# Two units of the first MoE's hidden layer moved ahead of, and beside, the last attention head's product with v

## The chip, the core and the metric

The kernel runs on one core of a Trainium2 chip. The metric is the device time of one execution in microseconds (us). All times below are of this core; the profile's clock starts at the beginning of its span.

## What is computed

Sixteen heads of masked attention (queries and keys attend only within the same cluster), then two feed-forward layers on the 1536 x 512 result.

```python
def _attn_ref(q, k, v, centroids):
    ...
    mask = q_assign[:, :, :, None] == k_assign[:, :, None, :]
    scores = scale * np.matmul(q, k.transpose(0, 1, 3, 2))
    scores = np.where(mask, scores, -1000000000.0)
    ...
    return np.matmul(attn, v)

def _moe_ref(x, w_in, w_out, a, b):
    h = x @ w_in
    P = a[0] + a[1] * h + a[2] * h2 + a[3] * h3
    Q = 1.0 + np.abs(b[0]) * np.abs(h) + np.abs(b[1]) * h2
    return (P / (Q + 1e-06)) @ w_out
```

`_moe2_ref` follows (a matmul, a softmax-weighted activation, a layer norm, a matmul). q, k and v have shape (2, 8, 768, 64); the first MoE goes 512 -> 2048 -> 512, the second 512 -> 1024 -> 512. The weights come as 64-bit floats, which the kernel turns into 32-bit ones on the way.

## The kernel before

**Attention.** Each of the 16 heads has six units of 128 query rows. A unit is a pair of score products in a two-bank PSUM tile of the tag `s` (two such tiles take turns), a minimum on VectorE (DVE, L384), an exponential on ScalarE (ACT, L397); every second unit a 32x32 block transpose on DVE (L414). The product with v (L424, 96 instructions of 64x192 a head, in a four-bank PSUM tile) of one head runs on TensorE (PE) among the units of the next. The last head has no next: its product stands alone at the end of attention. ACT copies each product out (`pv_out`, L440); that copy of head 14 must be done before head 15's product may write the same banks. For the last pair of heads the reciprocals of the row sums are spread by DVE (`rw`, L454) and turned by six PE transposes (`rbp`, L457); DVE then scales the result into `XF` (L476, L490). `XF[0..2]` are three blocks of 512 tokens; block 0 belongs to the first batch element and is complete before the last head ends.

**First MoE.** Every operand of its products is a sum of two parts, `h` and `l`, so that one product is three PE instructions: (w_h, x_h), (w_h, x_l), (w_l, x_h). A block of x is split into `XH` by four ACT copies (L325) and into `XL` by four subtractions (L612, GpSimd (POOL) for block 0). Unit u of 48 is one block of 512 tokens and one strip f of 128 of the 2048 hidden columns: `ff_h` makes h with 12 PE instructions of 128x512 (L717) in one of four PSUM banks of tag `t`; `ff_g1`, `ff_g2`, `ff_g3` put the rational function on it: ACT (L730, L731), POOL (L732, L733), DVE (L734, L735), ACT ln and exp (L741, L742), DVE (L744, L745, L746), ACT and POOL for the parts `gh` and `gl` (L751, L752). ln and exp write into h's own bank, so this bank comes free after L746. `ff_y` (L769, 12 PE instructions) adds the unit to y, which lies in both `s` tiles. Unit u + 4 needs the bank of unit u.

**Weights on the way.** Strips 0 to 4 of w_in are prepared during attention, strips 5 to 11 during units 0 to 8. A half strip is called by its strip and half here (strip 5: w50 and w51): a DMA into `raww` (SyncE's (SP) queue, L116), one ACT step (L126), a pair of DVE steps (L129, L131), then the parts `w1h` (ACT, L135) and `w1l` (POOL, L136). `raww` lies in the space of the last head's p and v, so its first DMA waits for that head's product.

**Order.** The calls are written in program order, and a scheduler in the build sets the order of each engine's queue from them; within a queue instructions start in order. `behind` adds an edge that fixes the order of two instructions on one engine. A tile is tracked as a whole: who reads one bank of a two-bank tile may be made to wait for who used the other.

Of the kernel before, what the change touches and what calls it, by code (L numbers as in the profile page):

```python
# [7 lines left out]
F32 = mybir.dt.float32  # L8
F32R = mybir.dt.float32r
# [21 lines left out]
def fused_kernel(ctx: ExitStack, tc: tile.TileContext, qT, kT, v, cent, w1, w2i, w2o, gln, coef, centT, cst, out):  # L31
# [385 lines left out]
    def pv_step(n, i):  # L417
        if i == 0:
            pv[n] = psum4(f"pv{n}")
        for c in range(2):  # L420
            j = 2 * i + c
            for r in range(4):
                sl = slice(32 * r, 32 * r + 32)
                last["pv"] = nc.tensor.matmul(  # L424
                    pv[n][64 * c:64 * c + 64, r, 0:192].rearrange("p (t q) -> p t q", t=NT),
                    lhsT=vv[n][sl, j], rhs=PT[n][sl, :, 32 * j:32 * j + 32],
                    start=(i == 0), stop=(i == S // 64 - 1),
                )

    U, W = {}, {}  # L430

# [185 lines left out]
    for idx, (n, t) in enumerate(units):  # L617
        if idx == ACL:
            asg.close()
            wh["r"] = ctx.enter_context(tc.tile_pool(name="wh2", bufs=4, side="right"))  # L620
        for k in range(3, len(sets)):
            if idx == AT[k] - LD:
                load_pairs(sets[k])
        if t == 0:
            if n + 2 < B * H:
                load_head(n + 2)
            if n >= 1 and n + 1 < B * H:
                spread(prep_head(n + 1), 7, idx, idx + 6)
        if t == 2:
            load_v(n)  # L630
        sp = unit_scores(n, t)
        m = unit_max(n, t, sp)
        if t % 2 and idx > 1:
            turn_p(*divmod(idx // 2 - 1, NT // 2))
        if idx == S1A:
            set1_a()
        if idx == S1B:
            set1_b()

        if n and t >= 3:  # L640
            for i in range(4 * (t - 3), 4 * (t - 2)):
                pv_step(n - 1, i)
            if t == 5 and n % 2 == 0:
                pair_sums(n // 2 - 1)
        unit_exp(n, t, sp, m)
        if n >= 2 and t < 2:
            pv_out(n - 2, t)
            if t == 1 and n % 2:

                fin_ = pair_fin(n // 2 - 1)  # L650
                for i in (1, 5, 6, 7):
                    plan[min(96, idx + i)].append(fin_)
        run_plan(idx)
    for i in range(2):
        pv_out(B * H - 2, i)
    turn_p(B * H - 1, NT // 2 - 1)
    pair_sums(B * H // 2 - 1)
    for i in range(NS):
        pv_step(B * H - 1, i)
    for i in range(2):  # L660
        pv_out(B * H - 1, i)
    XHL = xy.tile([128, 9, 512], F32R, name="xhl", tag="x")
    XH, XL = XHL[:, 0:4], XHL[:, 4:8]
    for _ in split_x(0, nc.scalar, nc.gpsimd):
        pass
    for _ in pair_fin(B * H // 2 - 1):
        pass
    for _ in range(3):
# [37 lines left out]
    def ff_h(u):  # L706
        j, f = ff_units[u]
        xh, xl = XH, XL
        w_h, w_l = w1_t[f]
        if u and u % 8 == 0 and (f == 0 or j < 2):  # L710
            for _ in split_x(j, nc.scalar, nc.vector):
                pass
        hp = psum1(f"h{u}")
        i = 0
        for kt in range(4):
            for w, x in ((w_h, xh), (w_h, xl), (w_l, xh)):
                r = nc.tensor.matmul(hp, lhsT=w[:, kt * 128:(kt + 1) * 128], rhs=x[:, kt], start=(i == 0), stop=(i == 11))  # L717
                if u < 4 and i == 0:
                    behind(r, last["pv"])
                i += 1  # L720
        return hp
# [267 lines left out]
```

## Time and profile before

| what | us |
|---|---|
| median of 3 runs | 711.69 |
| lowest and highest run | 710.28, 712.29 |
| the profiled execution's own time | 711.83 |
| its span in the profile | 710.0 |
| PE busy in the span | 617.8 (87%) |
| DVE busy | 528.8 (74%) |
| ACT busy | 409.6 (58%) |
| POOL busy | 399.5 (56%) |

The span is what the profile shows from the first instruction to the last; 1.8 us of the profiled execution lie around it. Matmuls are pipelined, so a busy PE is not PE at its peak. The chain that ended last lies on PE for 39% of the span, on DVE for 13%, on POOL for 3%, on ACT for 2% and on DMA for 1%. The granted clock of TensorE has two levels, 2.4 GHz (1.00 in the rows) and 1.2 GHz (0.50). The stretch that the change touches goes from 257 us, where the last exponential ends, to about 300 us.

### The profile page before, as it was taken

The page shows a single profiled execution, that of the slowest core. Times are in us where ns is not written, and L with a number is a line of the kernel's source. Part 1 is how long each engine was busy: PE and PEld are TensorE (multiplying, and loading weights), DVE is VectorE, ACT ScalarE, POOL GpSimd, SP SyncE. Part 2 cuts the span into 40 slices and gives each one's busy share as a digit, 9 for nine tenths or more (in the row PEclk, how much of TensorE's full clock was granted, in tenths as well). Part 3 has the DMA queues.
Part 4 walks back from the last instruction along what each step waited for, and adds up shares of the span by engine and source line. Part 5 has one row for each costly group of instructions (what it writes and reads, how often), then busy time and mean ns, then how long its engine had stood idle before and what let it go on. Part 6 is the DMA issues. An engine that isn't in the chain of part 4 may idle for free.

```text
span 710.0 us, 13783 instructions
## 1 busy us (share of the span) xinstructions
PE 617.8 (87%) x5517; PEld 487.6 (69%) x5517; DVE 528.8 (74%) x695; ACT 409.6 (58%) x748; POOL 399.5 (56%) x363
## 2 busy tenths in 40 slices
PE   6777876687688778599999999899979999999998
PEld 3555655565466556478788878678858888888887
DVE  4779798898978854999866999987677765444450
ACT  2536554665557644887757777758556544444341
POOL 8555447383758743999856999897669500000000
PEclk9779999899789889799999999999989999999999
DMA  9964393855747304323100234230010000000001
GB/s 258 257 168 102 91 257 112 209 144 142 178 127 173 85 25 159 137 90 120 60 1 0 87 120 124 87 118 1 0 31 0 1 1 15 31 30 15 18 28 44
DMA packets 22439, 64.71 MB, mean 91 GB/s; under 512 B 4532, under 2 KB 5640, under 8 KB 22376
## 3 DMA queue, kind: packets, MB, share of 16 engines
q1 hardware_dynamic: 21944, 63.67, 32.0%
q8 instruction: 43, 0.70, 0.4%
q10 hardware_dynamic: 432, 0.17, 0.1%
q14 instruction: 20, 0.16, 0.1%
HBM read 59.16 MB, written 3.19 MB: 88 GB/s over the span
## 4 chain that ended last, share of the span: by engine, by line
PE 39%; DVE 13%; issue 4%; POOL 3%; ACT 2%; DMA 1%; SPq 0%; ACTq 0%; POOLq 0%; DVEq 0%
PE y L769 10%; PE o L896 9%; PE hh L845 9%; PE h L717 8%; DVE y L734 2%; DVE w1w L131 2%; DVE q L744 2%; DVE h L745 2%; PE lt L878 1%; DVE y L746 1%; DVE y L735 1%; DVE w1w L129 1%; DVE xhl L612 1%; POOL q L733 1%; DMA raww<-in_w 1%
## 5 line engine op out<-in xcount | busy, mean ns | idle before, releaser
L717 PE MATMUL h<-xhl,w1h 128*128 128x512 f32 x384 | 126.8, 406 | 20.5 <-DVE y L746 17.3
L397 ACT ACTIVATE p<-s,m 128x768 f32<-128x768 f32 x96 | 86.0, 898 | 83.1 <-DVE m L384 82.6
L384 DVE TENSOR_REDUCE m<-s 128x1 f32<-128x768 f32 x96 | 89.0, 942 | 30.2 <-PE s L379 29.9
L373 PE MATMUL s<-k,q 128*128 128x384 f32 x192 | 63.8, 418 | 48.1 <-ACT p L397 47.6
L717 PEld LDWEIGHTS h<-xhl,w1h 128*128 128x128 f32 x384 | 74.2, 195 | 40.9 <-DVE y L746 20.1
L424 PE MATMUL pv<-pt,v 32*64 32x192 f32 x3072 | 86.8, 363 | 3.1 <-issue 2.9
L414 DVE STREAM_TRANSPOSE pt<-p 128x1536 f32<-128x1536 f32 x48 | 84.5, 1762 | 0.0
L373 PEld LDWEIGHTS s<-k,q 128*128 128x128 f32 x192 | 33.1, 210 | 72.7 <-ACT p L397 55.2
L424 PEld LDWEIGHTS pv<-pt,v 32*64 32x64 f32 x3072 | 65.9, 148 | 20.6 <-issue 15.2
L769 PE MATMUL y<-gl,w1h 128*128 128x512 f32 x192 | 75.6, 394 | 1.5 <-POOL gl L752 1.5
L717 PE MATMUL h<-xhl,w1l 128*128 128x512 f32 x192 | 76.5, 400 | 0.0
L752 POOL TENSOR_TENSOR gl<-y,gh 128x512 fp32r<-128x512 f32 x48 | 66.9, 1393 | 14.7 <-ACT gh L751 14.6
L769 PE MATMUL y<-gh,w1l 128*128 128x512 f32 x192 | 75.1, 391 | 0.0
L769 PE MATMUL y<-gh,w1h 128*128 128x512 f32 x192 | 68.7, 392 | 0.2 <-ACT yp L785 0.2
L733 POOL TENSOR_TENSOR q<-q,t 128x512 f32<-128x512 f32 x48 | 66.7, 1389 | 2.8
L732 POOL TENSOR_SCALAR q<-t,ab 128x512 f32<-128x512 f32 x48 | 48.4, 1009 | 27.6 <-ACT t L730 18.8
L379 PE MATMUL s<-k,q 128*128 128x384 f32 x192 | 55.9, 378 | 2.3 <-DVE k L575 2.3
L741 ACT ACTIVATE h<-q,qc 128x512 f32<-128x512 f32 x48 | 33.2, 692 | 36.6 <-POOL q L733 29.0
L734 DVE TENSOR_TENSOR y<-y,h 128x512 f32<-128x512 f32 x48 | 32.7, 680 | 28.4 <-ACT y L731 28.3
L845 PE MATMUL hh<-vh,xhl 128*128 128x512 f32 x192 | 53.2, 391 | 0.0
L490 POOL TENSOR_TENSOR xf<-u,rb 128x512 f32<-128x512 f32 (+1 forms) x14 | 13.9, 1016 | 64.2 <-DMA rb<-rd 64.2
L769 PEld LDWEIGHTS y<-gl,w1h 128*128 128x128 f32 x192 | 36.1, 188 | 10.7 <-POOL gl L752 2.9
(151 smaller groups left out, 1358.4 us busy)
## 6 DMA issues: line engine op xcount, KB each, us to landing
raww<-in_w SPq DMA_DIRECT2D x32, 512.0 KB, 4.2
v<-in_v SPq DMA_DIRECT2D x64, 192.0 KB, 4.7
dup<-in_qT SPq DMA_DIRECT2D x31, 192.0 KB, 5.6
dup<-in_kT SPq DMA_DIRECT2D x31, 192.0 KB, 5.1
rawv<-in_w2i SPq DMA_DIRECT2D x8, 512.0 KB, 3.7
rawv<-in_w2o SPq DMA_DIRECT2D x8, 512.0 KB, 4.0
out<-ob SPq DMA_DIRECT2D x11, 256.0 KB, 2.0
pr<-in_qT SPq DMA_DIRECT2D x7, 384.0 KB, 6.0
```

The lines of the kernel that those rows point to most:

```text
L373: r = nc.tensor.matmul(sp[:, a, 0:384], lhsT=q1[i][:, sl], rhs=k1[i][:, a * 384:(a + 1) * 384], start=True, stop=False)
L379: last["pe"] = nc.tensor.matmul(sp[:, a, 0:384], lhsT=q2[i][:, sl], rhs=k2[i][:, a * 384:(a + 1) * 384], start=False, stop=True)
L384: last["dve"] = nc.vector.tensor_reduce(m, sp[:, :, 0:384], axis=AX.XY, op=ALU.min)
L397: last["act"] = nc.scalar.activation(out=P[n, t // 2][:, t % 2], in_=sp[:, :, 0:384], func=AF.Exp, scale=-1.0, bias=m, accum_out=rs[key][: ...
L414: r = nc.vector.transpose(PT[n][:, 2 * i:2 * i + 2].rearrange("p t k -> p (t k)"), p.rearrange("p t a k -> p (t a k)"))
L424: last["pv"] = nc.tensor.matmul(pv[n][64 * c:64 * c + 64, r, 0:192].rearrange("p (t q) -> p t q", t=NT), lhsT=vv[n][sl, j], rhs=PT[n][sl, ...
L717: r = nc.tensor.matmul(hp, lhsT=w[:, kt * 128:(kt + 1) * 128], rhs=x[:, kt], start=(i == 0), stop=(i == 11))
L733: nc.gpsimd.tensor_tensor(q, q, t, op=ALU.mult)
L752: nc.gpsimd.tensor_tensor(gl, y, gh.bitcast(F32), op=ALU.subtract)
L769: nc.tensor.matmul(o, lhsT=w[:, c], rhs=g, start=(first and i == 0), stop=(last and i == 2))
L845: last["th"] = nc.tensor.matmul(hp[:, a], lhsT=y[:, kt], rhs=w[:, 512 * a:512 * a + 512], start=(kt == 0 and e == 0), stop=(kt == 3 and e ...
L896: r = nc.tensor.matmul(op[:, 0:m], lhsT=l[:, kt], rhs=w, start=(n == 0), stop=(n == 23))
```

## The change

The h of units 0 and 1 goes into one two-bank tile of tag `s`, called `early`, instead of two `t` banks. Block 0 of x is split right after the last unit, ahead of the copies of head 14's product; half of the `XL` subtractions go from POOL to DVE. The eight products of unit 0 with `XH` are put ahead of the last head's product with v, its four products with `XL` and the 12 of unit 1 behind it. `pair_sums`, which makes `rw` and `rbp`, is written behind them. In `ff_h`, units 0 and 1 return the bank that is already filled, and the edge to the last product with v now holds for units up to 5.

```diff
     def pv_step(n, i):
...
+        before = last["pv"] if i == 0 and n == B * H - 1 else None
...
+                if before:
+                    behind(last["pv"], before)
+                    before = None
...
+    XHL = xy.tile([128, 9, 512], F32R, name="xhl", tag="x")
+    XH, XL = XHL[:, 0:4], XHL[:, 4:8]
+    early = psum2("s", "h01")
+
+    def early_h(u, i0, i1):
+        w_h, w_l = w1_t[u]
+        ps_ = [(w, XH, kt) for kt in range(4) for w in (w_h, w_l)] + [(w_h, XL, kt) for kt in range(4)]
+        for i in range(i0, i1):
+            w, x, kt = ps_[i]
+            r = nc.tensor.matmul(early[:, u], lhsT=w[:, kt * 128:(kt + 1) * 128], rhs=x[:, kt], start=(i == 0), stop=(i == 11))
+            behind(r, last["pv"])
+            last["pv"] = r
+
+    for kt in range(4):
+        rnd(nc.scalar, XH[:, kt], XF[0][:, kt])
+    early_h(0, 0, 8)
     for i in range(2):
         pv_out(B * H - 2, i)
     turn_p(B * H - 1, NT // 2 - 1)
-    pair_sums(B * H // 2 - 1)
+    for kt in range(4):
+        (nc.gpsimd, nc.vector)[kt // 2].tensor_tensor(XL[:, kt], XF[0][:, kt], XH[:, kt].bitcast(F32), op=ALU.subtract)
     for i in range(NS):
         pv_step(B * H - 1, i)
+    early_h(0, 8, 12)
+    pair_sums(B * H // 2 - 1)
     for i in range(2):
         pv_out(B * H - 1, i)
-    XHL = xy.tile([128, 9, 512], F32R, name="xhl", tag="x")
-    XH, XL = XHL[:, 0:4], XHL[:, 4:8]
-    for _ in split_x(0, nc.scalar, nc.gpsimd):
-        pass
+    early_h(1, 0, 12)
...
+        if u < 2:
+            return early[:, u]
...
-                if u < 4 and i == 0:
+                if u < 6 and i == 0:
                     behind(r, last["pv"])
```

On PE, at the end of attention, the queue before reads as follows (`pv14`, `pv15` are the products of heads 14 and 15, `h0` the h of unit 0; what a row waits for stands in brackets, by the engine or DMA semaphore):

```order
L424 MATMUL pv14_3165<-pt14_2985,v14_2960 64x192 x32
L457 MATMUL rbp_3290<-cst_70,rw_3288 128x128 [waits DVE_49,Activation_49]
L457 MATMUL rbp_3290<-cst_70,rw_3288 128x128 x5
L424 MATMUL pv15_3297<-pt15_3163,v15_3141 64x192 [waits DMAHW3_49,PE_49,Activation_49]
...
L424 MATMUL pv15_3297<-pt15_3163,v15_3141 64x192 x92
L717 MATMUL h0_3465<-xhl_3396,w1h0_2537 128x512 [waits PE_49,Activation_49]
```

and with the change (`h01` is the tile `early`):

```order
L425 MATMUL pv14_3165<-pt14_2985,v14_2960 64x192 x32
L669 MATMUL h01_3282<-xhl_3281,w1h0_2537 128x512 [waits Activation_49]
L669 MATMUL h01_3282<-xhl_3281,w1l0_2538 128x512
L461 MATMUL rbp_3409<-cst_70,rw_3407 128x128 [waits DVE_49,PE_49]
L461 MATMUL rbp_3409<-cst_70,rw_3407 128x128 x5
L669 MATMUL h01_3282<-xhl_3281,w1h0_2537 128x512 [waits Activation_49]
L669 MATMUL h01_3282<-xhl_3281,w1l0_2538 128x512
...
L425 MATMUL pv15_3304<-pt15_3163,v15_3141 64x192 [waits DMAHW3_49,PE_49,Activation_49]
...
L425 MATMUL pv15_3304<-pt15_3163,v15_3141 64x192 x92
L669 MATMUL h01_3282<-xhl_3281,w1h0_2537 128x512 [waits Pool_49] x2
```

Two of the eight early products stand ahead of the transposes `rbp`, six stand between these and head 15's product, and the rest of units 0 and 1 behind it.

On ACT, at the start of the first MoE, the queue before reads (`t0`, `y0` are the first two ACT steps of unit 0, `t1` the first of unit 1; `h0<-q0` and `h0<-h0` are ln and exp of unit 0):

```order
L126 ACTIVATE w1w51_3487<-raww151_3488 128x512 [waits DMAHW3_49]
...
L126 ACTIVATE w1w60_3528<-raww160_3529 128x512 [waits DMAHW4_49,Pool_49]
L730 ACTIVATE t0_3478<-h0_3465 128x512 [waits DMAHW1_49,DMAHW5_49,DMAHW0_49,PE_49]
L731 ACTIVATE y0_3480<-h0_3465,coef_72 128x512
...
L730 ACTIVATE t1_3513<-h1_3500 128x512 [waits PE_49,Activation_49,Pool_49]
L731 ACTIVATE y1_3515<-h1_3500,coef_72 128x512
L741 ACTIVATE h0_3465<-q0_3479,qc_3449 128x512 [waits DVE_49]
...
L742 ACTIVATE h0_3465<-h0_3465 128x512 [waits Activation_49]
```

and with the change:

```order
L126 ACTIVATE w1w51_3499<-raww151_3500 128x512 [waits DMAHW3_49]
L135 ACTIVATE w1h5_3480<-w1w50_3482 128x512 [waits DMAHW5_49,DMAHW4_49,DMAHW6_49,DMAHW1_49,DMAHW7_49,DMAHW0_49,DVE_49]
L754 ACTIVATE t0_3490<-h01_3282 128x512 [waits DMAHW0_49,DMAHW1_49,PE_49,DMAHW5_49,Activation_49,Pool_49]
...
L765 ACTIVATE h01_3282<-q0_3491,qc_3474 128x512 [waits Pool_49]
L135 ACTIVATE w1h6_3525<-w1w61_3580 128x512 [waits DVE_49]
L766 ACTIVATE h01_3282<-h01_3282 128x512 [waits Activation_49]
...
L135 ACTIVATE w1h7_3631<-w1w70_3633 128x512 [waits DVE_49]
L754 ACTIVATE t1_3512<-h01_3282 128x512 [waits DVE_49]
L755 ACTIVATE y1_3514<-h01_3282,coef_72 128x512
L775 ACTIVATE gh0_3521<-y0_3492 128x512
```

`t0` has moved ahead of w60's step; `t1` has moved from ahead of unit 0's ln to behind its exp and behind the DVE steps of w70. The DVE instruction that `t1` waits for is L770 of unit 0 (L746 in the kernel before), the last of that unit on DVE.

## Rows read from the trace of the kernel before

**Rows 1.** Busy time by stretch: us, busy us (instructions) of each engine, clock, DMA.

```profile
280.00:300.00 20.00, 11.35 (x43) 8.89 (x42) 19.67 (x27) 16.11 (x28) 18.28 (x15) 0.74 0.40 134
300.00:346.00 46.00, 43.69 (x187) 34.28 (x185) 44.15 (x60) 34.35 (x59) 43.52 (x33) 1.00 0.32 110
```

**Rows 2.** The chain that ended last, in order of time: start, us, what.

```profile
263.14 6.43 PE pv L424 x192
...
269.98 6.53 DMA raww<-in_w
...
282.17 0.68 DVE y L734
...
312.51 1.04 DVE xhl L612
...
467.48 2.73 PE h L717 x12
```

**Rows 3.** PE's timeline: start, us, instruction, count [idle before, what ended it].

```profile
255.25 1.56 PE L424 MATMUL pv<-pt,v 32*64 32x192 f32 x64
261.62 1.51 PE L457 MATMUL rbp<-cst,rw 128*128 128x128 f32 x6 [4.82 <-DVE rw L454]
...
291.20 1.22 PE L717 MATMUL h<-xhl,w1h 128*128 128x512 f32 x2 [8.65 <-DVE y L746]
...
292.65 1.05 PE L717 MATMUL h<-xhl,w1h 128*128 128x512 f32 x2
...
293.93 1.05 PE L717 MATMUL h<-xhl,w1h 128*128 128x512 f32 x2
...
301.73 0.62 PE L717 MATMUL h<-xhl,w1h 128*128 128x512 f32 x2
```

**Rows 4.** PE alone by stretch: us, busy us (instructions), granted clock, DMA.

```profile
260.00:261.00 1.00, 0.00 (x0) 0.93 0.00 0
267.00:268.00 1.00, 1.00 (x47) 0.66 0.00 0
284.00:285.00 1.00, 0.00 (x0) 0.88 0.85 303
```

**Rows 5.** ACT's timeline.

```profile
257.58 0.79 ACT L440 ACTIVATE u<-pv 64x768 f32<-64x768 f32 x1
...
259.10 2.17 ACT L325 ACTIVATE xhl<-xf 128x512 fp32r<-128x512 f32 x4
...
276.53 0.66 ACT L126 ACTIVATE w1w<-raww 128x512 f32<-128x512 f32 x1 [1.72 <-DMA raww<-in_w]
...
280.13 0.58 ACT L730 ACTIVATE t<-h 128x512 f32<-128x512 f32 x1
...
283.42 0.60 ACT L730 ACTIVATE t<-h 128x512 f32<-128x512 f32 x1 [0.50 <-POOL q L733]
```

**Rows 6.** DVE's timeline.

```profile
290.41 0.73 DVE L746 SCALAR_TENSOR_TENSOR y<-y,coef,h 128x512 f32<-128x512 f32 x1
...
295.35 0.73 DVE L746 SCALAR_TENSOR_TENSOR y<-y,coef,h 128x512 f32<-128x512 f32 x1
...
299.24 0.73 DVE L746 SCALAR_TENSOR_TENSOR y<-y,coef,h 128x512 f32<-128x512 f32 x1
...
303.77 0.67 DVE L744 SCALAR_TENSOR_TENSOR q<-q,h 128x512 f32<-128x512 f32 x1
304.37 0.73 DVE L735 SCALAR_TENSOR_TENSOR y<-y,coef,h 128x512 f32<-128x512 f32 x1
305.03 0.68 DVE L745 SCALAR_TENSOR_TENSOR h<-q,h 128x512 f32<-128x512 f32 x1
...
311.78 0.73 DVE L746 SCALAR_TENSOR_TENSOR y<-y,coef,h 128x512 f32<-128x512 f32 x1
```

**Rows 7.** POOL's timeline.

```profile
281.80 1.58 POOL L733 TENSOR_TENSOR q<-q,t 128x512 f32<-128x512 f32 x1
...
293.40 1.47 POOL L752 TENSOR_TENSOR gl<-y,gh 128x512 fp32r<-128x512 f32 x1
```

## The prediction

> **What bounds the kernel now.** First the busy time by stretch. From 280 to 300 us DVE is busy 19.67 of 20 us and PE 11.35; from 300 to 346 both are nearly full, PE 43.69 and DVE 44.15 of 46 [rows 1]. So early in the first MoE, PE has time to spare, and soon neither has. Then the chain of waits: the last head's product with v (263.14 to 269.57), the DMA of half strips of weights (the second lands at 276.51), then DVE instruction after instruction past 312.51 [rows 2]. PE's own rows show what the change aims at: a gap of 4.82 us before `rbp`, and one of 8.65 us before unit 4's h at 291.20, which waits for unit 0's L746, the last reader of its bank [rows 3].
>
> What the reader should see: the filled gaps are PE's, while the chain runs over the DMA and DVE. PE work moved into a gap is worth only what it makes DVE do earlier.
>
> **Part 1, up to the last product with v.** Before, ACT's two copies of head 14 stand ahead of the split, from 257.58; the four `XH` copies start at 259.10, one every 0.54 us (2.17 over 4) [rows 5]. With the order turned round the first `XH` is there at about 258.2 and the fourth at 259.8. Then come head 14's copies (1.52 us, from 257.58 to 259.10), done by 261.3, before anybody needs them. Two early products run at 258.3. The third stands behind `rbp`, which starts at 261.62 and ends at 263.13 as before, for DVE's `rw` is not earlier [rows 3]. So 4.8 us of gap take only 0.5 us of work; six products fall between `rbp` and head 15.
>
> Their price depends on the clock. In 260 to 261 the granted share is 0.93, so it fell to the lower level at 260.86; in 267 to 268 it is 0.66, so it rose at 267.68 [rows 4]. At the lower level the products of this shape go one in 0.43 us (three from 292.65 to 293.93 [rows 3]), so six take 2.56; at the upper one 0.23 (12 in 2.73 [rows 2]), so 1.37. I take the lower level: PE stands nearly idle in that gap still. Head 15 then starts at 265.69. Of its product 1.9 us lay after the rise before; at 24.4 ns each (64 in 1.56 [rows 3]) that is 77 of the 192. From 265.69 to 267.68 some 51 are done at the slow pace (115 in 4.54 us), and 141 at 24.4 ns take 3.44. End: 271.1 instead of 269.57, **+1.6 us**.
>
> The first weight DMA waits for that end, and so the second lands at 278.1. SP's queue has the same order as before.
>
> **Part 2, unit 0.** The remaining 16 products end at 274.8. In front of `t0` ACT has w51's first step at the landing (278.1 to 278.8) and one copy, so `t0` starts at 279.2, against 280.13 [rows 5], though all inputs are later: it passed w60's step in the queue. L758 (L734 before) starts on DVE at 280.45, against 282.17 [rows 2], 1.7 us earlier. But it passed a DVE pair too. From 282.17 to 312.51 DVE ran 41 instructions in 30.34 us: 16 at 0.60 and 11 at 0.66 (the distances of starts in [rows 6]), 16.9 us, and seven pairs in the other 13.5, so 1.93 a pair. Passing one leaves **+0.2 us**.
>
> **Part 3, the wait that comes in.** `t1` now waits for unit 0's last DVE instruction, and it stands on ACT behind unit 0's exp. Followed through the queues: on POOL w51's subtraction stands between the two steps of q; it starts behind w51's copy (281.0) and q's first step and ends at about 283.0, and at 1.4 to 1.6 us a step [rows 7] q is ready at 284.4, against 283.38. On ACT the exp stands behind w61's copy, which needs DVE until 285.8 (two pairs behind L759 at 281.8); the exp ends at 287.0, and DVE stands idle for 1.25 us. With two strip steps in between, unit 0 leaves DVE at 291.8, against 291.14 [rows 6]. `t1` starts there, against 283.42 [rows 5]. Behind it ln waits for POOL's q, which waits for `t1`; DVE idles for another 0.3, 0.45 and 0.2 us. Unit 1 leaves DVE at 300.9, unit 2 at 307.0, unit 4 at 317.0, against 296.08, 299.97 and 312.51 [rows 6]. Not all of that is loss, since DVE has done strip work meanwhile: at unit 4's end one pair more, 1.93 us, is behind it, so the lag is 2.6, and the idle time alone says **+2.2 us** on top of part 2.
>
> This term was never measured. Its lower end is 0 (`t1` delayed, but DVE always has strips to do), its upper end 4.8 (unit 1's lag in full). I take 2.2, nearest to the counted idle time.
>
> Here the Trainium skill speaks against me. Its page "PSUM — Partial Sum Buffer" (section "Specifications (TRN2)") says ScalarE and VectorE can access PSUM in parallel at full rate as long as there is no bank collision, and h of units 0 and 1 lie in two banks; by it the term would be 0 and the sum +0.2. No run here shows that; the wait stands in the order, so the rule has no hold on it.
>
> **PE's side, as a check.** Unit 6's h needs the bank of unit 2: 307.0 instead of 301.73 [rows 3], with ten more products of y done by then (2.3 us): +3.0. Units 4 and 5 did run early, up to 286.7, but `ff_y` of unit 0 waits for `gl`, 296.2 instead of 294.87 [rows 7], and its second half for the tile `early`, so for unit 1, until 300.9. The gap is moved, not closed.
>
> **Edits at no cost.** Two subtractions on DVE after `rw` lie in time that DVE spent waiting for head 15's copies; at 0.67 each, as its other steps of this shape [rows 6], they would cost 1.3 us without that cover. POOL keeps two of four, so it is done earlier. Head 15's copies and the scaling into `XF` are 1.6 us later, and nothing reads these before block 1's split at 312.51 [rows 2]. The wait of the next h for the copies is hidden behind 16 products (3.7 us). The wider edge (up to unit 5) only fixes an order that holds anyway.
>
> **Sum.** 0.2 + 2.2 = 2.4 on DVE's side, 3.0 on PE's; I take 2.6, since the chain runs on DVE first. Behind that both are as full as before, so nothing gives it back. 711.83 + 2.6 = 714.4 against the profiled execution, 714.3 against the median of the runs, which is 0.14 lower. Farther on the scheduler has also changed many places by one or two instructions; I cost that at nothing and bound it by one pair, 1.9 us, either way. About 0.3% (2.1 us) is what a measurement of this kernel tells from no change.
>
> **Rivals.**
> *The clock holds* (0.18). The two early products at 258.3 break the gap, and it may be that the clock stays up. For it: before, PE did nothing at all there. Against: it also fell at 284.76, with the share at 0.88 from 284 to 285 [rows 4], 2.2 us after products that had kept PE full. Then head 15 starts at 264.5 and ends after 4.7 us at 269.2, 1.9 us earlier than in part 1: 714.4 - 1.9 = 712.5. In the words of the Trainium skill ("TensorE: Matmul & The Clock Gate", section "Part 1: The HAM clock gate (the "warmup" mystery)") the slow state is the default and activity releases it, by which either can come; no run here shows it.
>
> *PE was the bound, and the gap does close* (0.15, the other side). From 300 to 346 PE has 2.3 us to spare [rows 1]; with the h of units 4 and 5 taken out, 5.5 us, DVE alone sets the pace. It gains the 1.7 us of an earlier L758 and its own 1.85 us of idle time: 711.83 - 3.55 = 708.3. It decides at unit 1: if that leaves DVE by 296 as before, this holds. Against it is the place of `t1` in the queue.
>
> *No change* (0.15). The delay is there, but the units after the last strip take it back, since DVE has time again there: 711.8. Against: in 300 to 346 POOL is as full as PE (43.52 us [rows 1]), and both wait for the late units.
>
> **Numbers.** Forecast 0.52, at 712.9 to 717.5. Its upper end is 711.83 + 0.2 + 4.8 and some 0.7 of the later places; the lower end of all that is no gain on DVE's side is 711.83 - 1.9, about 710. Range 710.0 to 717.5; most of the faster rival lies below it. Slower by over 2.1 us: four fifths of the forecast and a little of the clock's case, 0.46. Faster: 0.14. The rest, 0.40, within 0.3%.
>
> **What would show it.** Right: the last product with v ends near 271, the clock is at 0.50 at 262; DVE's first L758 at 280 to 281; `t1` after unit 0's L770, at 291 to 292; unit 1's L770 at 300 to 301; PE idle from 287 to 293 and again before 301. Wrong: unit 1's L770 before 297, or the product with v ending by 269.5, or DVE idle for less than 1 us from 281 to 308.

## The result and the profile after

The changed kernel takes 720.79 us (median of 4 runs, 716.05 to 721.42), the kernel before on the same chip 711.52 (4 runs, 710.28 to 712.29). The ratio is 1.0114 with a 95% interval of 1.0081 to 1.0148; by the medians it is 9.3 us more. The forecast was 2.6 us more, with a range up to 717.5.

| us | before | after |
|---|---|---|
| the profiled execution | 711.83 | 721.42 |
| its span | 710.0 | 719.6 |
| PE busy, share of the span | 617.8, 87% | 624.3, 87% |
| DVE busy | 528.8 | 532.8 |
| ACT busy | 409.6 | 408.8 |
| POOL busy | 399.5 | 393.5 |
| the row that closes the last exp starts at | 257.14 | 259.17 |
| from there to the end of the span | 452.9 | 460.4 |

The last two lines matter for every date below. Up to the last exp no instruction moved, and still it closed 2.03 us later in this profile. In the 17 profiles of this study that row starts anywhere from 254.95 to 261.18. So dates are counted from it here, and times are compared by ratios. Even so two profiles of one order differ: from that row to the end the change takes 460.4 and, run again (e1), 461.9 us, the kernel before 452.9 and, with the same order written out (e15), 451.1. A difference of under 2 us between two profiles shows nothing by itself.

First the stretches that answer to [rows 1], 2 us later as the last exp is. The columns are the window, its length, then busy time and instructions of PE, its weight loads, DVE, ACT and POOL, the granted clock, the DMA share and GB/s.

```profile
282.00:302.00 20.00, 8.86 (x28) 5.99 (x28) 18.49 (x23) 13.47 (x23) 16.14 (x13) 0.71 0.42 143
302.00:348.00 46.00, 41.74 (x169) 32.58 (x168) 43.68 (x60) 34.93 (x60) 41.75 (x33) 0.94 0.31 104
```

PE was meant to gain here. It is busy 8.86 of 20 us instead of 11.35, since its early work is done and the next waits; DVE lost 1.2 us.

PE's own rows, which answer to [rows 3] (start, length, what ran, and in brackets the idle time before it and what ended it):

```profile
260.28 0.50 PE L669 MATMUL h<-xhl,w1h 128*128 128x512 f32 x1 [1.45 <-ACT xhl L325]
...
263.38 1.51 PE L461 MATMUL rbp<-cst,rw 128*128 128x128 f32 x6 [2.36 <-DVE rw L458]
264.54 0.78 PE L669 MATMUL h<-xhl,w1h 128*128 128x512 f32 x1
...
266.93 4.27 PE L425 MATMUL pv<-pt,v 32*64 32x192 f32 x192
...
292.80 0.80 PE L793 MATMUL y<-gh,w1h 128*128 128x512 f32 x1 [6.72 <-ACT gh L775]
295.90 0.80 PE L793 MATMUL y<-gl,w1h 128*128 128x512 f32 x1 [2.31 <-POOL gl L776]
300.52 0.80 PE L793 MATMUL y<-gh,w1h 128*128 128x512 f32 x1 [2.12 <-DVE y L770]
307.64 0.73 PE L741 MATMUL h<-xhl,w1h 128*128 128x512 f32 x2 [1.16 <-DVE y L770]
```

The gap of 8.65 us before unit 4's h is gone and has come back as 6.72 + 2.31 + 2.12 us before y of units 0 and 1. From the end of the product of head 14 (its last rows start at 257.28) to 302 us PE is idle 14.95 us of 44.72, before, from 255.25 to 300, 15.27 of 44.75. The early products moved PE's idle time and did not lessen it.

ACT's and DVE's rows on the way there, which answer to [rows 5] and [rows 6]; first ACT:

```profile
279.06 0.59 ACT L754 ACTIVATE t<-h 128x512 f32<-128x512 f32 x1
...
290.96 0.60 ACT L754 ACTIVATE t<-h 128x512 f32<-128x512 f32 x1 [0.41 <-DVE y L770]
```

and DVE:

```profile
280.35 0.69 DVE L758 TENSOR_TENSOR y<-y,h 128x512 f32<-128x512 f32 x1 [0.52 <-ACT y L755]
...
287.38 0.69 DVE L768 SCALAR_TENSOR_TENSOR q<-q,h 128x512 f32<-128x512 f32 x1 [1.33 <-ACT h L766]
...
290.19 0.74 DVE L770 SCALAR_TENSOR_TENSOR y<-y,coef,h 128x512 f32<-128x512 f32 x1
```

`t1` does start 0.03 us behind unit 0's last DVE step. Unit 4's last step ends at 316.57, which is 57.40 us behind the last exp, against 55.37 before: 2.0 us later, with one pair of strip steps more done (11 L131 steps by then, before 10). At unit 7 it is 2.7 us, again with one pair more. The rest of the loss comes later, and PE's rows there show some of it:

```profile
328.27 1.22 PE L741 MATMUL h<-xhl,w1h 128*128 128x512 f32 x2 [2.67 <-DVE y L770]
...
413.21 0.72 PE L741 MATMUL h<-xhl,w1h 128*128 128x512 f32 x2 [0.75 <-DVE y L770]
417.30 0.73 PE L741 MATMUL h<-xhl,w1h 128*128 128x512 f32 x2 [0.60 <-DVE y L770]
431.14 0.73 PE L741 MATMUL h<-xhl,w1h 128*128 128x512 f32 x2 [0.34 <-DVE y L770]
436.15 0.72 PE L741 MATMUL h<-xhl,w1h 128*128 128x512 f32 x2 [1.54 <-DVE y L770]
454.24 0.74 PE L741 MATMUL h<-xhl,w1h 128*128 128x512 f32 x2 [1.41 <-DVE y L770]
470.65 0.84 PE L741 MATMUL h<-xhl,w1h 128*128 128x512 f32 x2 [2.93 <-DVE y L770]
```

The six from 413 on add up to 7.57 us; before, the six gaps from 418 to 463 us add up to 4.61:

```profile
418.55 0.74 PE L717 MATMUL h<-xhl,w1h 128*128 128x512 f32 x2 [0.69 <-DVE y L746]
422.59 0.50 PE L769 MATMUL y<-gl,w1h 128*128 128x512 f32 x1 [0.53 <-POOL gl L752]
445.63 0.73 PE L717 MATMUL h<-xhl,w1h 128*128 128x512 f32 x2 [0.59 <-DVE y L746]
455.80 0.50 PE L717 MATMUL h<-xhl,w1h 128*128 128x512 f32 x1 [0.71 <-DVE xhl L612]
460.36 0.50 PE L717 MATMUL h<-xhl,w1h 128*128 128x512 f32 x1 [0.63 <-DVE xhl L612]
462.55 1.22 PE L717 MATMUL h<-xhl,w1h 128*128 128x512 f32 x2 [1.46 <-DVE y L746]
```

Nothing that the change names stands there. But the scheduler has put the later queues in another order, and that is the suspicion that the experiments follow.

### The profile page after: what moved, and what is told of

Its sections match the earlier page's. It is cut to its first block, busy times and chain, and to the rows that moved or that the text cites. A ratio compares the mean times of both kernels' runs of the same rounds, so it can differ in the third digit from the quotient of the medians.

```text
span 719.6 us, 13781 instructions
## 1 busy us (share of the span) xinstructions
PE 624.3 (87%) x5517; PEld 490.5 (68%) x5517; DVE 532.8 (74%) x697; ACT 408.8 (57%) x748; POOL 393.5 (55%) x361
## 4 chain that ended last, share of the span: by engine, by line
PE 40%; POOL 8%; DVE 8%; ACT 3%; issue 3%; DMA 1%; SPq 0%; ACTq 0%; POOLq 0%; DVEq 0%
PE y L793 10%; PE hh L869 9%; PE o L920 9%; PE h L741 9%; POOL q L757 2%; POOL gl L776 2%; PE lt L902 1%; POOL q L756 1%; POOL w1l L136 1%; DVE w1w L131 1%; POOL vl L136 1%; DVE q L768 1%; DVE xhl L616 1%; DMA raww<-in_w 1%; DVE y L770 1%
## 5 line engine op out<-in xcount | busy, mean ns | idle before, releaser
L741 PE MATMUL h<-xhl,w1h 128*128 128x512 f32 x368 | 119.3, 401 | 12.0 <-DVE y L770 12.0
L373 PE MATMUL s<-k,q 128*128 128x384 f32 x192 | 64.5, 422 | 48.4 <-ACT p L397 47.6
L741 PEld LDWEIGHTS h<-xhl,w1h 128*128 128x128 f32 x368 | 69.9, 192 | 31.0 <-DVE y L770 15.8
L425 PE MATMUL pv<-pt,v 32*64 32x192 f32 x3072 | 84.7, 356 | 2.3 <-issue 2.1
L793 PE MATMUL y<-gl,w1h 128*128 128x512 f32 x192 | 77.8, 405 | 4.1 <-POOL gl L776 4.1
L793 PE MATMUL y<-gh,w1h 128*128 128x512 f32 x192 | 71.0, 403 | 11.8 <-ACT gh L775 9.7
L793 PE MATMUL y<-gh,w1l 128*128 128x512 f32 x192 | 76.8, 400 | 0.0
L741 PE MATMUL h<-xhl,w1l 128*128 128x512 f32 x184 | 72.9, 397 | 0.0
L757 POOL TENSOR_TENSOR q<-q,t 128x512 f32<-128x512 f32 x48 | 68.2, 1420 | 2.6
L756 POOL TENSOR_SCALAR q<-t,ab 128x512 f32<-128x512 f32 x48 | 45.4, 947 | 29.4 <-ACT t L754 22.4
L758 DVE TENSOR_TENSOR y<-y,h 128x512 f32<-128x512 f32 x48 | 32.7, 682 | 29.8 <-ACT y L755 29.7
L793 PEld LDWEIGHTS y<-gh,w1h 128*128 128x128 f32 x192 | 37.0, 193 | 21.3 <-ACT gh L775 10.5
```

Source lines behind the costliest of these rows:

```text
L373: r = nc.tensor.matmul(sp[:, a, 0:384], lhsT=q1[i][:, sl], rhs=k1[i][:, a * 384:(a + 1) * 384], start=True, stop=False)
L425: last["pv"] = nc.tensor.matmul(pv[n][64 * c:64 * c + 64, r, 0:192].rearrange("p (t q) -> p t q", t=NT), lhsT=vv[n][sl, j], rhs=PT[n][sl, ...
L757: nc.gpsimd.tensor_tensor(q, q, t, op=ALU.mult)
L793: nc.tensor.matmul(o, lhsT=w[:, c], rhs=g, start=(first and i == 0), stop=(last and i == 2))
```

## The experiments

Two theories to begin with. **A**: the early products and the wait of `t1` cost it, and later stages only pass the delay on. **B**: the early part costs what was forecast, and the rest is the new order of the units behind it. Beside them stands **C**: a part of it is chance in the attention stage. All ratios are to the kernel before, run beside.

| run | us | ratio | 95% interval |
|---|---|---|---|
| e1 the change again | 721.7 | 1.0156 | 1.0131 to 1.0180 |
| e2 no early products | 707.05 | 0.9943 | 0.9922 to 0.9963 |
| e3 unit 0 only | 715.68 | 1.0071 | 1.0049 to 1.0093 |
| e4 ln and exp to SBUF | 720.75 | 1.0135 | 1.0109 to 1.0160 |
| e5 the change, order of e2 | 709.18 | 0.9973 | 0.9950 to 0.9997 |
| e6 the change, order of before | 716.45 | 1.0055 | 1.0029 to 1.0081 |
| e7 e2, order of the change | 721.94 | 1.0154 | 1.0123 to 1.0185 |
| e8 before, order of e2 | 705.23 | 0.9904 | 0.9878 to 0.9930 |
| e9 unit 0 only, order of before | 714.74 | 1.0034 | 1.0013 to 1.0054 |
| e10 unit 0 only, order of e2 | 708.89 | 0.9951 | 0.9928 to 0.9975 |
| e11 six products behind | 717.66 | 1.0079 | 1.0051 to 1.0108 |
| e12 before, four DVE steps moved | 712.0 | 0.9998 | 0.9970 to 1.0026 |
| e13 order of before, units 8 to 15 | 718.51 | 1.0106 | 1.0072 to 1.0140 |
| e14 order of before, from 16 on | 716.63 | 1.0093 | 1.0057 to 1.0128 |
| e15 before, its order written out | 710.64 | 1.0000 | 0.9976 to 1.0023 |

**e1: the same again.** No edit.

> The changed kernel once more, nothing edited, for the spread of its time and of its stages. Theory A (the wait of t1 for unit 0 and what hangs on it set the loss) and theory B (the new order of instructions behind unit 7, which the scheduler chose, costs most of it) both expect 719 to 722 us, and the same idle times of TensorE as in the first profile: 6.7, 2.3 and 2.1 us before 302 us, and about 5 us more than before between 302 and 572. Theory C (part of the loss is chance: the attention stage took 2.0 us longer in the first profile though its order is unchanged) expects the last exp to start anywhere from 256 to 259 us and the time to move with it, with a median of 717 to 719.

721.7 us. Here the last exp closed 2.3 us earlier than in the first profile (256.89), but the rest took 461.9 us, so the time stayed. PE's gaps were 6.99, 2.19 and 2.13 us. Theory C is out as a cause of the loss.

**e2: no early products.** The other edits stay.

```diff
-    early_h(0, 0, 8)
...
-    early_h(0, 8, 12)
...
-    early_h(1, 0, 12)
...
-        if u < 2:
-            return early[:, u]
```

> The change without the early products: h of units 0 and 1 computed where they were before, in banks of their own, the other edits (block 0 of x split ahead of the copies, two subtractions on VectorE) kept. Theory A expects no loss: 711 to 713 us, t1 within 5 us of t0, unit 1's last VectorE step near 296 us. Theory B expects 715 to 718, because the scheduler orders the later units anew for this edit too, with TensorE idle 4 to 6 us more than before between 302 and 572.

Neither theory had this: 707.05, faster than before by 0.6%. Up to unit 7 it is level with the changed kernel (78.0 and 78.6 us behind the last exp), and then it wins 13.5 us. That spoke for B, with an order that can also be better than the one before. Up to unit 7 e2 is not level with the kernel before, though: that stood at 75.9 there, and at 74.3 to 75.6 in three more profiles with its early order (e8, e12, e15). The section on why the prediction failed comes back to this.

**e3: unit 0 only.**

```diff
-    early_h(1, 0, 12)
...
-        if u < 2:
+        if u < 1:
+            turn[0] += 1
             return early[:, u]
```

> The changed kernel with h of unit 0 alone in the score banks; unit 1 has a bank of its own as before, so t1 waits for nothing of unit 0. Theory A expects 712 to 715 us: t1 about 4 us behind t0, no idle VectorE from 281 to 308, unit 1's last VectorE step at 295 to 298 us. Theory B expects 716 to 720, with unit 1 as early as A says, and the loss behind 317 us.

715.68. ACT's rows: `t1` has a bank of its own and starts at 280.70, 3.5 us behind `t0`:

```profile
277.19 0.58 ACT L754 ACTIVATE t<-h 128x512 f32<-128x512 f32 x1
...
280.70 0.60 ACT L754 ACTIVATE t<-h 128x512 f32<-128x512 f32 x1 [1.17 <-POOL q L757]
```

Unit 1's last DVE step ends 33.9 us behind the last exp (before 38.9), unit 5's 54.1 (before 63.5). A part of that lead is strip work put off (8 pairs done by unit 4, before 10), and all of it is gone at unit 20 (149.8, before 145.7). The dates are as B had them; the time lies between A's range and B's.

**e4: ln and exp into SBUF**, so that nobody writes over `early`.

```diff
         q, y, r = live[u]
+        if u < 2:
+            r = T("r", u)
```

> The changed kernel with both units early, but the result of ln and exp of units 0 and 1 written to a tile in SBUF instead of over h, so that t1 waits for nothing of unit 0 and the score banks come free with unit 1's second product on VectorE. Theory A expects a gain: 708 to 713 us, VectorE's idle time of 1.3 us gone, unit 1's last VectorE step by 297 us, y of units 0 and 1 begun by 296 us. Theory B expects 715 to 719 in spite of that.

720.75, no gain: above the ranges of both theories, and against A, though not a clean test of it. The wait for unit 0's last step is gone, but the scheduler leaves `t1` on ACT behind unit 0's ln, and DVE is idle for it as before. ACT:

```profile
283.80 0.71 ACT L767 ACTIVATE r<-q,qc 128x512 f32<-128x512 f32 x1
284.41 0.57 ACT L754 ACTIVATE t<-h 128x512 f32<-128x512 f32 x1
```

and DVE:

```profile
285.69 0.69 DVE L758 TENSOR_TENSOR y<-y,h 128x512 f32<-128x512 f32 x1 [1.40 <-ACT y L755]
```

**e5 to e8: the order by itself.** Everything from unit 7's ln on is written in the same sequence in all these kernels: 1680 matmuls, 401 DVE, 380 ACT, 158 POOL instructions and 42 DMAs. Their order in the queues can therefore be taken from one kernel and given to another, by an edge between neighbours on each engine that fixes the order and waits for nothing (the tables of numbers and their unpacking are left out; `p_` is the order of an engine, `l_` its instructions as written):

```diff
+        if u == 8:
+            mark[0] = len(nc.cur_bb.bb.instructions)
...
+        for i_ in nc.cur_bb.bb.instructions[mark[0]:]:
+            mine.setdefault(str(i_.engine).split(".")[-1], []).append(i_)
+        for e_, (n_, s_) in ORDER.items():
...
+            for a_, b_ in zip(p_, p_[1:]):
+                tc.add_manual_dep(l_[b_], l_[a_].name, mybir.DependencyInfo(mybir.DependencyClass.NoSync, mybir.DependencyReason.DATA), reason="order")
```

Between the changed kernel and e2, 556 of the matmuls, 193 DVE, 211 ACT and 89 POOL instructions stand in another place, and none of the DMAs.

> The changed kernel, early products and all; only the order of what is written from unit 7's ln on is fixed, on all five engines, to the order that the scheduler gave the kernel without early products (707 us). Theory B (the later order costs it) expects 705 to 710 us: up to unit 7 the two kernels had stood level (78.6 and 78.0 us behind the last exp), and from there each stage should last as in the kernel without early products. Theory A (the early products cost it, later stages only pass the delay on) expects 717 to 722, as the changed kernel.

> The changed kernel with the order of the kernel before from unit 7's ln on. Theory B expects what step by step was forecast for the early part alone: 711 to 715 us. Theory A expects 717 to 722.

> The kernel without early products (707 us), with the changed kernel's order from unit 7's ln on. Theory B expects the loss to move over to it: 717 to 722 us. Theory A expects 705 to 710.

> The kernel before, with the order of the kernel without early products from unit 7's ln on. Theory B expects a gain without any edit of the work: 704 to 709 us, TensorE's idle time before its last VectorE result at 529 us (4.7 us) gone. Theory A expects 710 to 713.

709.18, 716.45, 721.94 and 705.23. Three of the four lie in B's range and none in A's; e6 lies between the two. The changed kernel with e2's order is no slower than before, e2 with the changed kernel's order is as slow as the change, and the kernel before with e2's order is 1% faster than itself. The kernel before with the changed kernel's order was not run.

The dates show how. Each number is the end of that unit's last DVE step behind the row that closes the last exp; the last column is the end of the span.

| | unit 4 | unit 7 | unit 15 | unit 23 | unit 31 | unit 39 | unit 47 | end |
|---|---|---|---|---|---|---|---|---|
| before | 55.4 | 75.9 | 116.6 | 166.6 | 213.7 | 258.5 | 307.5 | 452.9 |
| after | 57.4 | 78.6 | 120.2 | 171.9 | 222.2 | 263.1 | 308.1 | 460.4 |
| e6 | 57.9 | 79.3 | 120.0 | 170.1 | 217.2 | 262.0 | 311.2 | 456.7 |
| e5 | 56.6 | 78.5 | 118.6 | 165.1 | 219.3 | 257.3 | 300.3 | 448.5 |
| e2 | 57.1 | 78.0 | 116.0 | 163.0 | 217.3 | 255.2 | 298.3 | 446.3 |
| e7 | 54.6 | 79.7 | 122.5 | 174.2 | 224.5 | 266.7 | 311.7 | 462.9 |
| e8 | 53.4 | 74.9 | 115.2 | 161.6 | 215.9 | 253.9 | 296.9 | 445.0 |

e6 reads the early part apart from the later order: with the order of before it is 3.5 us behind at unit 7, 3.5 at unit 23, 3.7 at unit 47 and 3.8 at the end. Against e15, the other profile of that order, it is 5.0, 5.0, 5.3 and 5.6. So a delay from the early part passes through unchanged, neither taken back nor grown, and its size is known to some 2 us. And with one order a stage lasts the same whatever came ahead. From unit 23 to 31 and from 31 to 39, before:

```profile
423.74:470.86 47.12, 43.73 (x181) 34.21 (x180) 44.86 (x64) 35.13 (x61) 43.01 (x34) 0.96 0.38 112
470.86:515.59 44.73, 44.73 (x197) 36.57 (x196) 33.04 (x49) 28.93 (x48) 32.66 (x28) 1.00 0.08 24
```

e6, the order of before:

```profile
426.99:474.11 47.12, 43.73 (x180) 34.10 (x179) 44.89 (x64) 35.16 (x61) 43.01 (x34) 0.96 0.37 112
474.11:518.91 44.80, 44.80 (x197) 36.77 (x197) 33.22 (x49) 28.96 (x48) 32.65 (x28) 1.00 0.08 24
```

after, in its own order:

```profile
431.09:481.35 50.26, 44.33 (x184) 35.41 (x185) 49.47 (x64) 35.89 (x63) 46.55 (x37) 0.97 0.38 112
481.35:522.27 40.92, 40.92 (x181) 33.64 (x180) 31.41 (x47) 29.68 (x51) 29.38 (x26) 1.00 0.06 18
```

Between two orders the dates of units do not say where time is lost, since the work between them differs: the second of these stages is 3.8 us shorter after the change, with 181 PE instructions in it instead of 197, and at unit 47 the change is 0.6 us behind, with 727 PE instructions still to come instead of 697. PE's idle time says it. From the last exp to the end every kernel here has the same 2046 PE instructions. The sums over that stretch (its length, then busy time of each engine) are, for before, e6, after and e5:

```profile
sum 452.86, PE 423.06 PEld 344.75 DVE 315.80 ACT 268.27 POOL 242.68; mean PE 47.01 PEld 38.31 DVE 35.09 ACT 29.81 POOL 26.96
sum 456.69, PE 426.15 PEld 345.46 DVE 316.90 ACT 267.69 POOL 237.31; mean PE 47.35 PEld 38.38 DVE 35.21 ACT 29.74 POOL 26.37
sum 460.43, PE 425.95 PEld 345.88 DVE 321.86 ACT 267.61 POOL 236.74; mean PE 47.33 PEld 38.43 DVE 35.76 ACT 29.73 POOL 26.30
sum 448.47, PE 420.88 PEld 343.37 DVE 321.20 ACT 267.98 POOL 236.06; mean PE 46.76 PEld 38.15 DVE 35.69 ACT 29.78 POOL 26.23
```

From e6 to after, PE's busy time stays (426.15 and 425.95) and its idle time grows from 30.5 to 34.5 us (35.0 in e1): what the changed kernel's later order costs is 4 us of idle PE. From e6 to e5 PE has 3.0 us less idle time and 5.3 less busy time, at a granted clock of 0.97 and 0.98. From before to e6 idle time goes from 29.8 to 30.5 and busy time grows by 3.1 (against e15, by 2.5 and 3.0): a good part of what the early part costs is PE's work at the lower clock. From unit 0's last DVE step to unit 4's the granted clock is 0.91 before and 0.69 in e6 (columns as at the top):

```profile
291.14:312.51 21.37, 21.31 (x85) 17.38 (x86) 21.30 (x31) 16.96 (x29) 21.18 (x16) 0.91 0.33 113
290.37:314.85 24.48, 18.11 (x57) 13.12 (x58) 24.11 (x33) 19.23 (x33) 23.87 (x20) 0.69 0.38 126
```

In the stage from unit 23 to 31 DVE has 64 instructions in both orders, but they take 49.47 us instead of 44.86. DVE's groups in it, before and after, say which (busy time, mean ns of one, idle time):

```profile
L131 DVE SCALAR_TENSOR_TENSOR vw<-rawv,vw 128x512 uint32<-128x512 uint32 x10 | 10.1, 1013 | 0.0
```

```profile
L131 DVE SCALAR_TENSOR_TENSOR vw<-rawv,vw 128x512 uint32<-128x512 uint32 x10 | 13.4, 1341 | 0.1
```

The same ten steps take 3.3 us more. The stage is 3.1 us longer, and the six PE gaps from 413 us on add up to 3.0 us more. That the steps make the gaps is not shown: e5 has as much busy DVE time as the change (321.20 and 321.86) and is fast. Why ten equal steps differ stands in the last section.

**e9 and e10: the shared tile by itself**, e3 with the order of before and with that of e2.

> Only unit 0 early, unit 1 in a bank of its own, with the order of the kernel before from unit 7's ln on; to be set against both units early at that order (716.5 us, 3.8 us behind before in the profile). If the forecast's third part is right (t1 waits for unit 0, because the two units share one tile), that delay goes with the shared tile: 711 to 713 us, unit 4's last VectorE step 51 to 53 us behind the last exp instead of 57.9. If the delay has another cause in the early part (weight pairs passed, the clock), it stays: 715 to 718.

> Only unit 0 early, with the order of the kernel without early products from unit 7's ln on; both units early at that order took 709.2 us. If the shared tile is what costs: 704 to 707. If not: 708 to 711.

714.74 lies just under the range for another cause, 708.89 in it: both above what was expected if the tile were all of it. Unit 4 did leave DVE 50.7 us behind the last exp, about as expected, instead of e6's 57.9, but with 8 pairs of strip steps done instead of 10; at unit 7, with 14 pairs in both, 2.6 us of these 7.2 were left, and 2.8 at the end (453.9 against 456.7). By the ratios the second unit in the shared tile costs 1.5 us at the order of before (1.0055 and 1.0034) and 1.6 at e2's (0.9973 and 0.9951), both with intervals that overlap. So it is a part of the early loss at most, and not shown to be the larger one.

**e11: six products behind.**

```diff
-    early_h(0, 0, 8)
+    early_h(0, 0, 2)
...
-    early_h(0, 8, 12)
+    early_h(0, 2, 12)
```

> The changed kernel with the six early products between the transposes of rbp and the last product with v moved behind it; the later order is almost that of the changed kernel. The forecast's first part (six products at the lower clock delay the product with v by 1.6 us) expects 719 to 720 us against 720.8 to 721.7. By the first profiles, where the product with v ended no later after the last exp than before (12.1 us against 12.4), no difference: 720 to 722.

717.66. By the ratios that is 2.5 us under the change, with intervals that overlap, and 5.5 under e1, with intervals that do not; the time is under both ranges of the line. Its later order is the changed kernel's but for some 20 places on PE. PE's rows:

```profile
262.64 1.45 PE L461 MATMUL rbp<-cst,rw 128*128 128x128 f32 x6 [2.36 <-DVE rw L458]
264.02 5.16 PE L425 MATMUL pv<-pt,v 32*64 32x192 f32 x192
```

The product with v ends 10.7 us behind the last exp. With the six ahead of it, it ended 12.0 to 12.7 us behind in ten profiles; without any early product and with the split first (e2, e7), 10.7. So against a kernel with the split first they delay it by 1.3 to 2.0 us, which has the forecast's 1.6 in it. Against the kernel before, where the split comes later, it is less: there the product ended 12.3 us behind the last exp in the profile shown and 11.3 to 11.5 in three others of the same early order (e8, e12, e15), so that the middle of the ten is 0.9 us later than the middle of the four. The argument from the first pair of profiles, that there was no delay, fell: in the profile shown of before that product took 6.39 us, in the three others 5.40 to 5.58.

**e12: four DVE steps of the order.** In before's order PE waits 4.74 us, until 529.52, for unit 40's last DVE step. VectorE's queue there, before and in e12, with the unit in brackets (L789 is block 1's y, taken out of its banks):

```
before  L744(40) L789     L735(41) L745(40) L789     L734(42) L746(40)
e12     L744(40) L745(40) L746(40) L735(41) L789     L734(42) L789
```

> The kernel before with its own order from unit 7's ln on, but on VectorE four instructions (both subtractions of block 1's y, one step each of units 41 and 42) stand behind the three last steps of unit 40, which TensorE waits for at 529.5 us. If the order of a few instructions there is what TensorE's idle time of 4.7 us hangs on, the step ends about 3.4 us earlier: 707 to 708 us, and down to 704 if the clock then does not fall. If other engines set that date, or the time is lost again later: 710 to 712.

712.0, no difference. The step came 3.4 us earlier, as expected (268.9 us behind the last exp, before 272.3), and PE's gap there shrank to 1.49. But unit 47 ended only 0.5 us earlier, and PE has a gap behind it that it had not before:

```profile
523.90 0.73 PE L718 MATMUL h<-xhl,w1h 128*128 128x512 f32 x2 [1.49 <-DVE y L747]
...
573.43 0.73 PE L846 MATMUL hh<-vh,xhl 128*128 128x512 f32 x2 [1.77 <-DVE yp L790]
```

So closing that one gap does not give what e2's order gains.

**e13 to e15: which half, and the price of writing out.** e13 and e14 give the changed kernel the order of before in one part of the units, and leave its own in the other; e15 gives the kernel before its own order.

> The changed kernel; what is written from unit 7's ln to unit 15's stands in the order of the kernel before, what is written later in the changed kernel's own. If the later loss sits where TensorE stood idle 2.7 us before unit 9's h (328 us; block 1's split ahead of unit 5's last steps on VectorE), it goes with that order: 718 to 719 us, and the idle time before 340 us is under 1 us. If it sits behind unit 15, 720 to 722.

> The other half: the changed kernel's own order up to unit 15's ln, that of the kernel before for what is written later. If the loss sits behind unit 15 (TensorE's idle time from 413 to 471 us, 7.6 us against 4.6): 717 to 718 us. If it sits ahead: 720 to 722. The two halves together took 716.5.

> The kernel before with its own order from unit 7's ln on written out, so that no instruction moves: what the writing out itself does. Every theory expects no difference, 710 to 713 us; if it differs by more than 2 us, the comparisons between written-out and free orders have to be read with that.

e15 shows no difference, so the comparisons stand. 718.51 lies in its line's range for a loss ahead of unit 15, 716.63 just under its line's range for one behind it. The ratios decide neither: 1.0106 for e13 is not clear of the change's 1.0114 or of e1's 1.0156, and 1.0093 for e14 is clear of e1's alone. The profiles say more. In e13 the idle time before 340 us did fall to under 1 us, as expected, but from the last exp on it takes 459.6 us with the gaps of 413 to 471 us still there (after 460.4, e1 461.9); e14 takes 457.0, which is e6's 456.7 but for 0.3. By the profiles most of the later loss sits behind unit 15; the times alone do not show it.

**The fastest** is e8, the kernel before with an order that the scheduler had found for another one: 705.23 us, 0.988 to 0.993 of before and faster than every version with early products.

## Why the prediction failed

Counted from the row that closes the last exp, the forecast's dates and those of the pair of profiles are:

| us behind the last exp | before | forecast | after |
|---|---|---|---|
| end of the last product with v | 12.3 | 14.0 | 12.0 |
| first L758 (before L734) | 25.0 | 23.3 | 21.2 |
| last DVE step of unit 0 | 34.0 | 34.7 | 31.8 |
| `t1` | 26.3 | 34.7 | 31.8 |
| last DVE step of unit 1 | 38.9 | 43.8 | 41.3 |
| of unit 2 | 42.8 | 49.9 | 48.4 |
| of unit 4 | 55.4 | 59.9 | 57.4 |

By the profile's own clock the product ended at 271.2, where 271.1 was forecast, L758 started at 280.35 and `t1` at 290.96, and all of it looks met. That is luck: this profile's last exp closed 2.03 us later than the one before.

**Part 1** (+1.6 us at the last product with v) has its cost right and the clock wrong. The six products took 2.4 us (264.54 to 266.93), where 2.56 was forecast, and against kernels with the split first they put 1.3 to 2.0 us on the product's end. But the forecast left the lower clock where it was before, from 260.86 to 267.68. In the profile after it fell at about 262.9 (from 262 to 263 us the granted share was still 0.95) and rose at about 266.3 (from 266 to 267 it was 0.84, then 1.00), before the product began. So no part of the product ran at the slow pace, and it took 4.27 us, before 6.39. In the ten profiles with the six ahead of it, it took 4.27 to 4.77 us, in the seven others 5.08 to 6.39. Against the kernel before, the end is 0.9 us later over the profiles and 0.3 earlier in the pair.

**Part 2** (L758 earlier, +0.2 by unit 0's end): L758 came 3.8 us earlier instead of 1.7, and unit 0 left DVE 2.2 us earlier instead of 0.7 later, mostly because part 1's delay was not there.

**Part 3** (t1 waits, DVE +2.2, and on PE's side +3.0) holds in what happens: `t1` starts behind unit 0's L770, DVE is idle 1.33 us for 1.25 ahead of it, though not again behind it, where 0.95 more was forecast, and from the product's end on every date of the table comes within 1 us of the forecast's distance. What it costs is less sure: e9 and e10 put 1.5 and 1.6 us on the second unit in the shared tile, with intervals that overlap, and e4 took the wait for unit 0's last step away and gained nothing. The Trainium skill ("PSUM — Partial Sum Buffer", section "Specifications (TRN2)") lets ScalarE and VectorE go to different banks at once, by which the term would be 0. Here `t1` did wait for L770, though its bank was another; no run here tried the banks alone.

**Edits at no cost** is not borne out. At e2's later order the kernel before takes 0.9904 (e8), the kernel with the other edits and no early product 0.9943 (e2), and the whole change 0.9973 (e5). By that the edits that were put at nothing, with the early order that came with them, cost 2.8 us, and the early products 2.1. The intervals overlap at both steps, e8's and e2's just; by the profiles it is 3.1 us at unit 7 from e8 to e2 (74.9 and 78.0) and 1.3 at the end (445.0 and 446.3). From the first L734 to unit 4's last step DVE never waits in e8; in e2 it waits four times, 4.2 us in all, each time for ACT. Which of these edits does it was not tried.

**The sum for the early part** was +2.6 us. At a fixed later order it is +3.9 by time (1.0055 of 711.5, with an interval of 2.1 to 5.8) at the order of before, and +4.9 at e2's (0.9973 to e8's 0.9904). At the changed kernel's own order the early products add nothing to e7 (1.0154 without them, 1.0114 and 1.0156 with them), so the price hangs on the order behind. The sign was right and the size lies within the first interval, but that it is made of the terms named is not shown: a part of it stands in the clock and in edits that were put at nothing.

**The step that failed** is the last one of the sum: "Farther on the scheduler has also changed many places by one or two instructions; I cost that at nothing and bound it by one pair, 1.9 us, either way." By the ratios it measured +4.2 us against the order of before (1.0114 to e6's 1.0055, with intervals that touch; +7.2 with e1's ratio, whose interval is clear of e6's) and +10 to +13 against that of e2 (e5). The bound was taken from one conversion pair. But against before 604 matmuls, 176 DVE, 184 ACT and 63 POOL instructions stand elsewhere, and in the profiles the new order leaves PE idle 4.0 us longer than the order of before does (after and e6). Which of the moved instructions do it stays open.

**The rivals.** The clock did not hold, as the share of 0.50 from 263 to 266 us shows; but its date for the product's end, 12.1 us behind the last exp, is nearer to the 12.0 measured than the forecast's 14.0. PE's gap did not close: its idle time up to 302 us stayed the same. No change was out.

## What to carry to other kernels

Where a scheduler orders the queues, every edit is two changes: the work, and a new order of all that follows; here, by the ratios, the second alone was worth 7 us on the kernel before (e8), 10 to 13 on the change (e5) and 15 on e2 (e7), and what the edits of the work cost at a fixed order was 5 at most. Measure an edit with the later order fixed (writing it out costs nothing, e15), at more than one order, since its price can differ between them, and give the forecast of a free one a range as wide as order alone has been seen to move the time. An order found for one variant can be the best for another, so the orders of all variants are worth trying on the fastest of them.

## What the runs showed of the hardware

**A DVE step on two SBUF operands can wait out POOL.** L131 takes 0.68 us with POOL idle (289.21 in the profile after, POOL idle from 288.41 to 290.63) and 1.67 beside it. The two rows, DVE and POOL of the profile after:

```profile
283.33 1.67 DVE L131 SCALAR_TENSOR_TENSOR w1w<-raww,w1w 128x512 uint32<-128x512 uint32 x1
```

```profile
282.97 1.48 POOL L757 TENSOR_TENSOR q<-q,t 128x512 f32<-128x512 f32 x1
```

It ends 0.55 us behind POOL's step. In the first MoE of that profile 10 L131 steps of 128x512 start with POOL idle, and none takes over 0.69 us; 28 start beside a POOL step, and 22 of these take over 0.75 and end behind it. Of L129, with one operand in SBUF, 10 and 25 of 28 do the same (0.41 to 0.43 us with POOL idle, up to 1.55 beside it). The 240 steps with an operand in PSUM keep 0.67 to 0.75 us whatever POOL does; in e4, where one of these operands went to SBUF, the first two such steps (`q<-q,r`) took 1.00 and 1.40, so e4 had a price of its own. Over the first MoE the 94 steps of L129, L131 and `XL` sum to 90.5 us in the profile after and 85.7 in e6, the same work in another order. The Trainium skill ("SBUF — State Buffer", section "SBUF: two separate sides") states that the two engines share a pair of ports by an exclusive lock for the whole instruction. The trace agrees: of the 22 stretched L131 steps and the 25 of L129 none ends before POOL's. That these 5 us make up the later loss is not shown; no run changed them alone, and e5 has 89.5 us of them and is fast.

**The same gap can cost the clock or not.** PE's gap of 2.67 us before unit 9's h is in the profile after (328.27) and in e14's:

```profile
326.88 0.74 PE L742 MATMUL h<-xhl,w1h 128*128 128x512 f32 x2 [2.67 <-DVE y L771]
```

Its two matmuls took 1.22 us in the first and 0.74 in the second; the granted clock of the stage from unit 4 to 7 was 0.92 and 1.00. In the same way the last product with v took from 5.40 to 6.39 us in the four profiles with before's early order. One profile of each kernel is not enough to price a microsecond there.
